# An attention-plus-MLP block rewritten: 512 attention units with 1024-wide exps over three PSUM pairs, one dense slot per unit, MLP in 352-token chunks

## The chip, the cores and the metric

The kernel runs on one core of a Trainium2 chip. The metric is device time of one execution in microseconds; several executions are timed, and the median is quoted. The profile is one execution, recorded by the hardware profiler.

In this text TensorE is PE in the profile (PEld is its weight load), VectorE is DVE, ScalarE is ACT, GpSimd is POOL, and SP issues most transfers. PSUM is the memory that TensorE writes to; the programs hold it as one tensor `ps` of eight banks of 512 columns. "Pitch" is the time from the start of one instruction to the start of the next. A shape like 128x512 is partitions by columns.

## The reference

```python
x = A_x                                   # 1 x 2048 x 1024, bf16
xn = layernorm(x)
# A: attention, 32 heads of 32
q, k, v = split(xn @ wqkv)                # wqkv 1024 x 3072
p = softmax(q @ k.T * 32 ** -0.5)         # 2048 x 2048 per head
s = (p @ v) @ wo                          # wo 1024 x 1024
# B: MLP on a second layernorm of xn
h = gelu(layernorm(xn) @ w1 + b1)         # w1 1024 x 3584, tanh form
g = silu(h @ w2 + b2)                     # w2 3584 x 1024
out = x + s * g
```

Both kernels cut attention into 512 units: four heads, 256 queries, 256 keys. A unit is eight score matmuls (S), the exps of 128 x 2048 scores, and sixteen matmuls for P·V and for the row sums (by a matrix of ones). The MLP and the Q/K/V projections ("dense work") are put between the units on TensorE, so that ScalarE, which has all the exps to do, is never left alone.

## The kernel before

It builds the instruction list of each engine by hand, with semaphore waits. One unit, and the filler of dense work:

```python
ACCB = 5                                   # bank of P.V and row sums
NRING = 5                                  # banks 0-4: scores; banks 6, 7: dense work
...
for kbh in range(2):
    for j in range(4):
        bk = (4 * b + j) % NRING
        ...
            w = [("act_exp", 4 * b - 1)]   # third exp of the unit before is done
        add("tensor", ... en.matmul(bank(bk, kbh * 256, (kbh + 1) * 256), lhsT=KT..., rhs=QT...), ...)
flush(act_pending, b)                      # tanh of earlier MLP items
for j in range(4):
    add("scalar", ... en.activation(Pb[b % NPB][:, j, :], bank(bk), ACT.Exp, scale=SCALE), ...)
if b >= 2:
    emit_pv(b - 2)
run_fillers(mlp_seq, per_batch_ns, None)   # as many dense matmuls as a time budget allows
flush(dve_pending, b)
```

At the end of each group of eight units (256 queries are finished) VectorE normalises straight out of the accumulator bank:

```python
add("vector", lambda en: en.reciprocal(rc_t[ri][:], ps[:, ACCB * 512 + 256:ACCB * 512 + 256 + QW]), ...)
add("vector", lambda en: en.tensor_tensor(OT[:, hg, qb * QW:(qb + 1) * QW],
                                          ps[:, ACCB * 512:ACCB * 512 + QW], rc_t[ri][:], op=ALU.mult), ...)
```

A first-layer MLP item is 256 tokens by two blocks of 128 hidden columns. Its gelu on VectorE: two evictions with bias, square, multiply-add, multiply, and (after tanh on ScalarE) one more; the evictions are 256 columns wide each, the rest 512.

```python
xb = bank + b1                             # L441, twice
u = xb * xb                                # L446
u = u * 0.044715 + 1                       # L448
u = u * xb                                 # L450
th = tanh(0.79788 * u)                     # ScalarE, L456
h = (th + 1) * xb                          # L461
```

The second layernorm's rows are transposed on TensorE and sent through DRAM; the gate is transposed back on TensorE.

The softmax here doesn't subtract the row's maximum and nothing guards it: scores larger than these inputs give would overflow.

## Time and profile before

| | before |
|---|---|
| device time, median of 3 | 1486.78 us |
| first exp starts | 107.0 us |
| 512 units, first exp to last | 1293 us (2.53 us a unit) |
| after the last exp | 86.0 us |
| records of the half-speed TensorE clock | 23, 117.7 us in all |

The first exp, the last and the clock records are read from single instruction times. They cut the run into three stretches. This is the view by windows of these three: the engines' busy time in each, with the granted clock, DMA share and GB/s at the end.

```profile
0.00:107.00 107.00, 54.78 (x652) 40.80 (x656) 57.26 (x113) 19.81 (x23) 32.97 (x38) 1.00 0.51 109
107.00:1400.00 1293.00, 1081.02 (x28992) 723.55 (x28984) 615.80 (x1015) 1121.68 (x2220) 23.08 (x32) 0.96 0.45 102
1400.00:1486.00 86.00, 70.06 (x698) 37.53 (x696) 29.11 (x45) 2.05 (x6) 46.68 (x50) 0.96 0.64 185
```

The columns are window, length, then PE, PEld, DVE, ACT, POOL. In the middle ScalarE is busy 1122 of 1293 us, and no engine is full. So the loss is in waits, spread over engines. The groups view shows what the main instructions cost (busy us, mean ns of one, then idle time of the engine before them and what ended it):

```profile
L695 ACT ACTIVATE Pb<-ps 128x512 bf16<-128x512 f32 x2048 | 1058.7, 609 | 173.2 <-PE ps L686 166.1
L302 PE MATMUL ps<-arena 128*32 128x256 bf16 x14336 | 494.0, 282 | 87.9 <-DMA arena<-in_B_w_dram 66.8
L612 DVE RECIPROCAL rc<-ps 128x256 f32<-128x256 f32 x64 | 112.4, 1756 | 145.8 <-PE ps L605 145.8
L446 DVE TENSOR_TENSOR arena<-arena 128x512 f32<-128x512 f32 x112 | 77.6, 693 | 12.4 <-DVE arena L441 0.9
```

L302 is a helper: its groups are told apart by their tiles; `arena` holds the MLP. ScalarE waits 166 us for scores, TensorE 66.8 us for weights. Twelve microseconds of ScalarE in time order, with idle time in brackets:

```profile
819.62 2.06 ACT L695 ACTIVATE Pb<-ps 128x512 bf16<-128x512 f32 x4
821.54 0.44 ACT L500 ACTIVATE arena<-arena 128x256 f32<-128x256 f32 x1
822.89 6.22 ACT L695 ACTIVATE Pb<-ps 128x512 bf16<-128x512 f32 x12 [0.91 <-PE ps L686]
828.97 0.44 ACT L500 ACTIVATE arena<-arena 128x256 f32<-128x256 f32 x1
829.89 2.06 ACT L695 ACTIVATE Pb<-ps 128x512 bf16<-128x512 f32 x4 [0.48 <-PE ps L686]
```

The best units take 2.06 to 2.08 us (822.89: three units in 6.22 us). Exps of one unit start 477 ns apart, so four take 1.91; the rest, about 155 ns, is the wait of each unit's first exp for scores that may start only after the third exp before.

The transfers of weights, with size and the median time from issue to landing:

```profile
arena<-in_B_w_dram SPq DMA_DIRECT2D x112, 512.0 KB, 4.0
arena<-in_B_w_dram SPq DMA_DIRECT2D x64, 896.0 KB, 6.9
```

### The profile page before, as it was taken

To read this page: it belongs to the slowest core of one execution; us is meant where nothing else is said; L and a number is where in the kernel's file an instruction comes from. 1 tells how busy PE (TensorE), PEld (TensorE's weight loads), DVE (VectorE), ACT (ScalarE), POOL (GpSimd) and SP (SyncE) were. 2 spreads that over 40 slices of the span, in tenths; PEclk is the share of its full clock that TensorE was granted. 3 is DMA by queue.
4 is the path that set the end of the run, shared out by engine and by line. 5 is a ranking of instruction groups with operands and counts; after the bars stand their busy time and mean duration, and the time that the engine had idled before them with its cause. 6 is when DMAs were issued, how large, how long until landed. Compare 5 with 4: busy or idle time off the path is not lost.

```text
span 1486.1 us, 65842 instructions
## 1 busy us (share of the span) xinstructions
PE 1205.9 (81%) x30330; PEld 801.9 (54%) x30336; DVE 702.2 (47%) x1173; ACT 1143.5 (77%) x2246; POOL 102.7 (7%) x119
## 2 busy tenths in 40 slices
PE   2589878887889878987798878988798878777887
PEld 1455656555556545565555555655455655555643
DVE  6532862257422772347522683238522682277233
ACT  1229988897889888988898989988898987687600
POOL 3320000000000100001000100001000000000057
PEclk9999999999999989999899999999999998998999
DMA  6350457125560556045524562165307556535764
GB/s 135 71 129 3 119 119 143 41 60 141 111 144 3 137 123 120 9 101 149 105 52 86 137 158 52 31 145 148 83 5 143 135 163 124 120 116 123 145 198 163
DMA packets 388676, 159.44 MB, mean 107 GB/s; under 512 B 255280, under 2 KB 378160, under 8 KB 388400
## 3 DMA queue, kind: packets, MB, share of 16 engines
q1 hardware_dynamic: 378640, 138.43, 40.6%
q0 software_dynamic: 9760, 16.80, 4.3%
q8 instruction: 238, 3.90, 1.1%
q14 instruction: 38, 0.31, 0.1%
HBM read 142.62 MB, written 12.58 MB: 104 GB/s over the span
## 4 chain that ended last, share of the span: by engine, by line
PE 40%; ACT 18%; DVE 17%; DMA 14%; issue 10%; POOL 1%; DVEq 0%; SPq 0%; ACTq 0%; POOLq 0%
ACT Pb L695 18%; PE ps L302 17%; DMA arena<-in_B_w_dram 13%; PE ps L686 7%; DVE rc L612 6%; PE ps L599 6%; PE ps L605 4%; PE ps L732 3%; DVE arena L441 3%; DVE arena L446 2%; PE ps L269 2%; DVE OT L614 1%; PE ps L383 1%; DVE arena L448 1%; DVE arena L450 1%
## 5 line engine op out<-in xcount | busy, mean ns | idle before, releaser
L695 ACT ACTIVATE Pb<-ps 128x512 bf16<-128x512 f32 x2048 | 1058.7, 609 | 173.2 <-PE ps L686 166.1
L302 PE MATMUL ps<-arena 128*32 128x256 bf16 x14336 | 494.0, 282 | 87.9 <-DMA arena<-in_B_w_dram 66.8
L302 PEld LDWEIGHTS ps<-arena 128*32 128x32 bf16 x14336 | 394.2, 100 | 129.7 <-issue 82.7
L599 PE MATMUL ps<-Pb,Vh 128*32 128x256 bf16 x4096 | 273.8, 285 | 47.9 <-DVE OT L614 38.5
L605 PE MATMUL ps<-Pb,ones 128*32 128x256 bf16 x4096 | 270.1, 281 | 7.8 <-issue 7.7
L686 PE MATMUL ps<-QT,KT 32*128 32x256 bf16 x4096 | 211.5, 280 | 74.5 <-ACT Pb L695 59.0
L599 PEld LDWEIGHTS ps<-Pb,Vh 128*32 128x32 bf16 x4096 | 110.2, 96 | 169.8 <-issue 111.8
L612 DVE RECIPROCAL rc<-ps 128x256 f32<-128x256 f32 x64 | 112.4, 1756 | 145.8 <-PE ps L605 145.8
L686 PEld LDWEIGHTS ps<-QT,KT 32*128 32x128 bf16 x4096 | 61.9, 93 | 219.4 <-ACT Pb L695 186.4
L494 DVE TENSOR_SCALAR arena<-ps,b2h 128x256 f32<-128x256 f32 x64 | 30.9, 482 | 271.9 <-PE ps L302 271.9
L302 PE MATMUL ps<-xnT,wsl 128*32 128x512 bf16 x2048 | 130.8, 388 | 2.1 <-DMA wsl<-in_A_wqkv_dram 2.1
L441 DVE TENSOR_SCALAR arena<-ps,b1T 128x256 f32<-128x256 f32 x224 | 97.9, 479 | 72.7 <-PE ps L302 70.6
L605 PEld LDWEIGHTS ps<-Pb,ones 128*32 128x32 bf16 x4096 | 112.1, 98 | 9.0 <-issue 6.4
L527 POOL DMA_DIRECT2D g_scratch<-arena x16 | 8.9, 558 | 1291.5 <-DVE arena L525 1291.1
L456 ACT ACTIVATE arena<-arena 128x512 f32<-128x512 f32 x112 | 72.3, 646 | 23.9 <-DVE arena L450 23.9
L446 DVE TENSOR_TENSOR arena<-arena 128x512 f32<-128x512 f32 x112 | 77.6, 693 | 12.4 <-DVE arena L441 0.9
L450 DVE TENSOR_TENSOR arena<-arena 128x512 f32<-128x512 f32 x112 | 77.6, 692 | 3.9
L302 PEld LDWEIGHTS ps<-xnT,wsl 128*32 128x32 bf16 x2048 | 55.3, 99 | 41.9 <-issue 6.8
L461 DVE SCALAR_TENSOR_TENSOR arena<-arena 128x512 bf16<-128x512 f32 x112 | 75.1, 685 | 3.4 <-ACT arena L456 3.1
L269 PE MATMUL ps<-ident,arena 128*128 128x128 bf16 x256 | 30.5, 312 | 49.3 <-DVE arena L256 49.3
L383 PE MATMUL ps<-wsl,xnT 128*128 128x128 bf16 x1024 | 67.8, 220 | 0.0
L383 PEld LDWEIGHTS ps<-wsl,xnT 128*128 128x128 bf16 x1024 | 57.4, 98 | 14.2 <-issue 13.8
(47 smaller groups left out, 520.2 us busy)
## 6 DMA issues: line engine op xcount, KB each, us to landing
arena<-in_B_w_dram SPq DMA_DIRECT2D x112, 512.0 KB, 4.0
arena<-in_B_w_dram SPq DMA_DIRECT2D x64, 896.0 KB, 6.9
wsl<-in_A_wqkv_dram POOLq DMA_DIRECT2D x24, 256.0 KB, 6.8
yT_scratch<-arena SPq DMA_DIRECT2D x16, 256.0 KB, 2.8
arena<-yT_scratch SPq DMA_DIRECT2D x8, 512.0 KB, 8.6
g_scratch<-arena POOLq DMA_DIRECT2D x16, 256.0 KB, 2.6
xnT<-in_A_x_dram SPq DMA_DIRECT2D x16, 256.0 KB, 3.0
xnT<-g_scratch SPq DMA_DIRECT2D x16, 256.0 KB, 3.8
```

What stands on the lines that cost most here:

```text
L302: add("tensor", lambda e, j=j: e.matmul(out_fn(j), lhsT=lhsT_fn(j), rhs=rhs, start=start, stop=stop, tile_position=(0, 32 * j), skip_group ...
L383: mms.append((lambda w, inc, DB, dc=dc, tb=tb, t4=t4: add("tensor", lambda e: e.matmul(bank(DB, t4 * 128, (t4 + 1) * 128), lhsT=xnT[:, dc, ...
L441: add("vector", lambda e, k=k, fb=fb: e.tensor_scalar(xb_t[gi][:, k * CW:(k + 1) * CW], bank(DB, k * CW, (k + 1) * CW), b1T[:, fb:fb + 1], ...
L446: add("vector", lambda e: e.tensor_tensor(u_t[gi][:], xb_t[gi][:], xb_t[gi][:], op=ALU.mult), waits=va, inc="gl_b")
L450: add("vector", lambda e: e.tensor_tensor(u_t[gi][:], u_t[gi][:], xb_t[gi][:], op=ALU.mult), waits=[("gl_b", sc.cnt("gl_b"))], inc="gl_u")
L456: add("scalar", lambda e: e.activation(th_t[gi][:], u_t[gi][:], ACT.Tanh, scale=0.7978845608028654), waits=[("gl_u", vu)], inc="gl_t")
L461: add("vector", lambda e: e.scalar_tensor_tensor(hT[:, pi * FBP:(pi + 1) * FBP, :], th_t[gi][:].rearrange("p (k t) -> p k t", k=FBP), 1.0, ...
L599: add("tensor", lambda en, j=j, kb=kb, kbh=kbh, firstg=firstg: en.matmul(ps[32 * j:32 * j + 32, ACCB * 512:ACCB * 512 + QW], lhsT=Vh[i2][: ...
L605: add("tensor", lambda en, j=j, kbh=kbh: en.matmul(ps[32 * j:32 * j + 32, ACCB * 512 + 256:ACCB * 512 + 256 + QW], lhsT=ones[:, 0:32], rhs ...
L612: add("vector", lambda en: en.reciprocal(rc_t[ri][:], ps[:, ACCB * 512 + 256:ACCB * 512 + 256 + QW]), waits=[("pe_pv", b + 1), ("dve_acc", ...
L686: add("tensor", lambda en, j=j, kb=kb, kbh=kbh, bk=bk, qb=qb, i2=i2: en.matmul(bank(bk, kbh * 256, (kbh + 1) * 256), lhsT=KT[i2][32 * j:32 ...
L695: add("scalar", lambda en, j=j, bk=bk, b=b: en.activation(Pb[b % NPB][:, j, :], bank(bk), ACT.Exp, scale=SCALE), waits=[("pe_s", b + 1), ( ...
```

## The change

The kernel was rewritten around a small scheduler that derives waits from named reads and writes. The intent: ScalarE does two wide exps per unit, and everything else is cut so that each unit carries exactly one piece of dense work. The diff is 1350 lines; its core, with cuts marked `...`:

```diff
-        ACCB = 5
-        NRING = 5
-                        bk = (4 * b + j) % NRING
+                bks.append(2 * ((2 * u + j // 2) % 3) + j % 2)      # three pairs of banks, 0-5
+        ACC = 6
+        state = {"bank": 7, "qi": 0}                                # one bank for dense work
...
-                for j in range(4):
-                    ... activation(Pb[b % NPB][:, j, :], bank(bk), ACT.Exp, scale=SCALE)
+            for p in range(2):
+                sl = (2 * u + p) % 3
+                op("scalar", ... activation(pb[:, 2 * p:2 * p + 2, :, :]..., ps[:, sl * 1024:(sl + 1) * 1024], ACT.Exp, scale=SCALE), ...)
...
-                ... en.reciprocal(rc_t[ri][:], ps[:, ACCB * 512 + 256:ACCB * 512 + 256 + QW])
-                ... en.tensor_tensor(OT..., ps[:, ACCB * 512:ACCB * 512 + QW], rc_t[ri][:], op=ALU.mult)
+                op("vector", lambda e: e.tensor_copy(a[:], bank(ACC)), ...)      # bank is free after this
+                for k in range(4):                                  # a quarter in each of four units
+                    dve_tasks[v + k].append(... e.reciprocal(rc[:, k * q4:(k + 1) * q4], a[:, QW + k * q4:...]))
+                dve_tasks[v + 3].append(... "gpsimd" ... e.tensor_tensor(OT..., a[:, 0:QW], rc[:], op=ALU.mult))
...
-    CW = 256
+    CW = 352                                                        # tokens of an MLP chunk
-    run_fillers(mlp_seq, per_batch_ns, None)
+    # one entry of the list per unit: a 128-column block of the first layer, a quarter of a
+    # second-layer item, a Q/K item, a V item or an output item
...
-    u = xb * xb; u = u * 0.044715 + 1; u = u * xb                   # VectorE, 512 wide
+    op("gpsimd", ... e.tensor_tensor(ub, xb, xb, op=ALU.mult))      # 352 wide
+    op("vector", ... e.scalar_tensor_tensor(ub, ub, 1.0 / 0.044715, xb, op0=ALU.add, op1=ALU.mult))
...
-    src = B_w1[:, pi * W1P:(pi + 1) * W1P]                          # 256 columns, 512 KB
-    src = B_w2[:, nb * 128:(nb + 1) * 128]                          # 896 KB
+    src = B_w1[:, k * 512:(k + 1) * 512]                            # 1 MB
+    src = B_w2[:, k * 256:(k + 1) * 256]                            # 1.8 MB
...
+    e.dma_start_transpose(yTc[:, :, 0:n], y_d[t0:t0 + n, :])        # no transposes of y on TensorE
+    e.dma_start_transpose(gres[i4]..., gT_d[:, lo:hi])              # nor of the gate
```

Some lines above are shortened to what they compute. The output projection (48 items) joins the same list, so part of it runs inside the last attention units.

## The prediction

> **What bounds it now.** From the trace's instruction times: first exp at 107.0 us, last ends at 1400.1. So three stretches: 107 us of layernorm and first projections, 1293 us for 512 attention units (2.53 us each), 86 us of tail. The groups view puts the exps (128x512 x2048) at 1058.7 us of busy ScalarE, 173 us idle before them. Start to start, exps of a unit follow at 477 ns, but a unit never takes under 2.08 us: five 512-column banks let the next scores start only after the unit's third exp, so at least 155 ns is lost per unit. Beyond that: every eighth unit 2.7-3.0 us (the 1756 ns reciprocal and 425 ns multiply hold the accumulator bank; 8.8% of the chain of waits in one 100 us window), units with tanh 2.44, and units up to 7.6 us where TensorE waits for weights (66.8 us in the waits view) or VectorE (gelu chain of four 512-wide steps). After each long wait the clock record shows half speed for 3.4 us or more.
>
> **What changes.**
> - Exps: 2 per unit, 1024 wide. A 1024-wide PSUM read on ScalarE took 1023 ns in this trace, a 512-wide exp 605 with pitch 477, so pitch about 905 (estimate), 1.81 us a unit instead of 2.08. The Trainium skill ("ScalarE: Activation LUTs", What ACT_TABLE_LOAD costs) gives 186 ns + 0.833 ns a column, less about 93 overlapped; the trace's pitch is 43 ns lower still. Three PSUM pairs let scores start after the first of the two exps: about 0.3 us slack, so the 155 ns loss goes.
> - TensorE: same columns. From the trace: 102-110 ns per 256-column quad, about 150 for 352. Scores 307, PV 409, dense slot 1.3 us (gelu or Q/K), 1.15 (quarter of w2), 0.92 (V). Unit 2.01, 1.86, 1.64.
> - VectorE: square moves to GpSimd, one step folded. Per w1 unit 0.58+0.53+0.53 us, plus four quarter reciprocals (about 0.55) and a 0.69 us copy per eight units: 2.1 us, also nearly full. Accumulator held 0.7 us instead of 2.2.
> - DMA: six weight passes instead of eight, 1 MB and 1.8 MB pieces with 4 or 8 slots lead, runs twice as long: landing 7 and 9-10 us (estimate from 4.0 and 6.9 us for half sizes) against about 8.6 and 15 us. Hidden.
> - y and gate transposed by DMA. No transposing DMA runs in this trace; "DMA: Bandwidth & Descriptors" (Latency and other measured facts) gives 261 GB/s, so about 3 us per chunk. Hidden unless several times slower.
>
> **Sum.** Per unit, the slower of ScalarE and TensorE: 168 w1 units at 2.15 (tanh adds 345 ns), 192 w2 at 1.9, 84 Q/K and 20 output at 2.01, 48 V at 1.81: 1021 us. Three engines nearly level with in-order queues and one dense bank: add 4%: 1062.
> Start: no y transposes on PE/VectorE, x in 8 queues; LN batches of about 10 us, last projections end near 70 us (now 107).
> Tail: 20 of 48 output items done earlier, no drained MLP: 28 x 1.2 us + PV and stores: 42 us (now 86).
> 70 + 1062 + 42 = about 1175.
>
> **Predicted: 1178 us, 1140 to 1245.** Faster by over 2%: 0.98; within: 0.015; slower: 0.005.
>
> **Right if:** exps 1024 wide, pitch about 905; ScalarE busy about 1000 us, over 90% in the middle; first exp 65-78 us; after the last exp 35-50 us; w1 units near 2.2, w2 near 1.9; DMA wait of matmuls under 20 us; few half-clock events.
> **Wrong if:** transposing DMAs take over 15 us and delay weights, or over 4 us each and bound the tail (they share one queue with in-order waits); VectorE is late with the single dense bank's eviction (w1 units 2.4+); GpSimd squares (1155 ns for 512 columns now) are slow next to VectorE.

## The result

| | before | after |
|---|---|---|
| device time, median of 4 | 1486.57 us | 1197.66 us |
| first exp starts | 107.0 us | 86.7 us |
| 512 units | 1293 us | 1069 us |
| after the last exp | 86.0 us | 37.3 us |
| half-speed clock records | 23, 117.7 us | 3, 8.0 us |

The ratio is 0.8084 (95% interval 0.8028 to 0.8140). Here and below a ratio compares one kernel's runs with those of the kernel before in the same rounds, so it is not quite the ratio of the medians quoted. The prediction of 1178 us, 1140 to 1245, held.

The windows of the three stretches after (columns as above):

```profile
0.00:87.00 87.00, 44.60 (x908) 31.66 (x912) 36.19 (x75) 27.62 (x42) 35.65 (x52) 0.96 0.57 149
87.00:1156.00 1069.00, 1023.12 (x27880) 633.99 (x27872) 595.39 (x1086) 1034.01 (x1240) 199.68 (x231) 1.00 0.38 104
1156.00:1193.00 37.00, 33.23 (x912) 24.72 (x912) 30.85 (x63) 0.00 (x0) 0.73 (x1) 1.00 0.66 163
```

ScalarE is busy 97% of the middle, and TensorE 96%. Of 293 us between the two profiles, 224 came from the middle, 49 from the tail, 20 from the start. The groups after:

```profile
L587 ACT ACTIVATE P<-ps 128x1024 bf16<-128x1024 f32 x1024 | 983.9, 1079 | 31.2 <-PE ps L575 22.0
L302 PE MATMUL ps<-yTc,war 128*32 128x352 bf16 (+1 forms) x5376 | 226.5, 308 | 14.5 <-DVE xb L392 6.9
L621 DVE RECIPROCAL rcs<-accs 128x64 f32<-128x64 f32 x256 | 133.3, 535 | 0.0
L396 DVE SCALAR_TENSOR_TENSOR u<-u,xb 128x352 f32<-128x352 f32 (+1 forms) x168 | 152.8, 909 | 0.0
L394 POOL TENSOR_TENSOR u<-xb 128x352 f32<-128x352 f32 (+1 forms) x168 | 150.0, 893 | 315.7 <-DVE xb L392 285.8
```

ScalarE's wait for scores fell from 166 to 22 us; the wait for weights is gone from these lines (the waits view has one, of 2.7 us). ScalarE in time order now runs without a bracket, tanh between exps:

```profile
154.77 1.95 ACT L587 ACTIVATE P<-ps 128x1024 bf16<-128x1024 f32 x2
156.58 0.53 ACT L399 ACTIVATE th<-u 128x352 f32<-128x352 f32 x1
156.97 1.97 ACT L587 ACTIVATE P<-ps 128x1024 bf16<-128x1024 f32 x2
158.77 0.55 ACT L399 ACTIVATE th<-u 128x352 f32<-128x352 f32 x1
159.16 1.99 ACT L587 ACTIVATE P<-ps 128x1024 bf16<-128x1024 f32 x2
```

Exps start 0.903 us apart (median of single instruction times), so a unit costs ScalarE 1.81 us, and 2.19 with a tanh. The transfers after:

```profile
war<-in_B_w_dram SPq DMA_DIRECT2D x42, 1024.0 KB, 5.4
war<-in_B_w_dram SPq DMA_DIRECT2D x24, 1792.0 KB, 9.4
xnT<-gT_scratch SPq DMA_TRANSPOSE x16, 4.8
yTc<-y_scratch SPq DMA_TRANSPOSE x6, 6.3
```

Twice the bytes land in 1.35 times the time, and a piece now lasts four or eight units.

The units can be sorted by the dense work that TensorE did in them, taking the time from a unit's first exp to the next unit's. Sums over all units of a kind, in us (mean of one in brackets):

| kernel | gelu (168) | second layer (192) | Q/K (84) | V (48) | output (19) |
|---|---|---|---|---|---|
| predicted | 361 (2.15) | 365 (1.9) | 169 (2.01) | 87 (1.81) | 38 (2.01) |
| after | 379 (2.26) | 385 (2.01) | 177 (2.11) | 87 (1.81) | 39 (2.04) |

The prediction added 4% to its sum for coupling and came to 1062 us; 1067 was measured from the first unit's first exp to the last unit's.

### The profile page after: what moved, and what is told of

It reads as the page before. It is cut to its first block, busy times and chain, and to the rows that moved or that the text cites. A ratio compares the mean times of both kernels' runs of the same rounds, so it can differ in the third digit from the quotient of the medians.

```text
span 1193.0 us, 62780 instructions
## 1 busy us (share of the span) xinstructions
PE 1100.9 (92%) x29696; PEld 690.4 (58%) x29696; DVE 662.4 (56%) x1223; ACT 1061.6 (89%) x1281; POOL 236.1 (20%) x284
## 4 chain that ended last, share of the span: by engine, by line
PE 67%; ACT 18%; DVE 10%; DMA 3%; issue 3%; POOL 0%; SPq 0%; POOLq 0%
PE ps L302 40%; ACT P L587 15%; PE ps L575 10%; PE ps L604 10%; PE ps L607 7%; DVE u L396 3%; DVE xb L392 2%; DVE hT L403 2%; ACT th L399 2%; DMA b2h<-in_B_b_dram 2%; DMA war<-in_B_w_dram 1%; ACT xnT L296 1%; DVE rcs L621 1%; DVE stats L245 1%; DVE accs L616 1%
## 5 line engine op out<-in xcount | busy, mean ns | idle before, releaser
L587 ACT ACTIVATE P<-ps 128x1024 bf16<-128x1024 f32 x1024 | 983.9, 1079 | 31.2 <-PE ps L575 22.0
L604 PE MATMUL ps<-P,VP 128*32 128x256 bf16 x4096 | 262.5, 278 | 4.9 <-DVE accs L616 4.2
L607 PE MATMUL ps<-P,ones 128*32 128x256 bf16 x4096 | 257.7, 273 | 3.0 <-issue 3.0
L302 PE MATMUL ps<-yTc,war 128*32 128x352 bf16 (+1 forms) x5376 | 226.5, 308 | 14.5 <-DVE xb L392 6.9
L302 PE MATMUL ps<-hT,war 128*32 128x352 bf16 (+1 forms) x5376 | 230.9, 308 | 8.5 <-issue 8.4
L394 POOL TENSOR_TENSOR u<-xb 128x352 f32<-128x352 f32 (+1 forms) x168 | 150.0, 893 | 315.7 <-DVE xb L392 285.8
L302 PEld LDWEIGHTS ps<-yTc,war 128*32 128x32 bf16 x5376 | 131.5, 96 | 72.6 <-DVE xb L392 16.8
L302 PEld LDWEIGHTS ps<-hT,war 128*32 128x32 bf16 x5376 | 142.1, 97 | 50.9 <-issue 12.0
L396 DVE SCALAR_TENSOR_TENSOR u<-u,xb 128x352 f32<-128x352 f32 (+1 forms) x168 | 152.8, 909 | 0.0
L302 PE MATMUL ps<-xnT,wq 128*32 128x352 bf16 (+2 forms) x2944 | 131.0, 320 | 10.3 <-ACT xnT L296 8.8
L621 DVE RECIPROCAL rcs<-accs 128x64 f32<-128x64 f32 x256 | 133.3, 535 | 0.0
L302 PEld LDWEIGHTS ps<-xnT,wq 128*32 128x32 bf16 x2944 | 77.2, 97 | 39.4 <-ACT xnT L296 8.1
```

Of the source, the lines that this page charges most:

```text
L302: ins = e.matmul(outs(j), lhsT=lhs(j), rhs=rhs, start=start, stop=stop, tile_position=(0, 32 * j), skip_group_check=True)
L394: op("gpsimd", lambda e: e.tensor_tensor(ub[:, 0:n], xb[:, 0:n], xb[:, 0:n], op=ALU.mult), r=[kx], w=[ku])
L396: "vector", lambda e: e.scalar_tensor_tensor(ub[:, 0:n], ub[:, 0:n], 1.0 / 0.044715, xb[:, 0:n], op0=ALU.add, op1=ALU.mult),
L587: op("scalar", lambda e, p=p, sl=sl: e.activation(pb[:, 2 * p:2 * p + 2, :, :].rearrange("p a b q -> p (a b q)"), ps[:, sl * 1024:(sl + 1) ...
L604: e.matmul(bankq(ACC, j, 0, QW), lhsT=VP[vp][:, kb, vo + 32 * j:vo + 32 * j + 32], rhs=pb[:, j, kh, :], start=first, stop=False, tile_posi ...
L607: ins = e.matmul(bankq(ACC, j, QW, 2 * QW), lhsT=ones[:, 0:32], rhs=pb[:, j, kh, :], start=False, stop=last, tile_position=(0, 32 * j), sk ...
```

## The experiments

All results agreed with the reference. The kernel with light weight loads computes with wrong MLP weights: the comparison does not see those weights. "Control" is the changed kernel again.

### Control

> The changed kernel as it is, on the chip that the other three share. Every theory: about 1197 us and a ratio to the kernel before of 0.80 to 0.815, first exp at 87 us, 1067 us of units, tail 37 us. It is the base from which the differences of the other three are taken.

Measured: 1195.88 us, ratio 0.8089 (0.8045 to 0.8132), first exp at 87.7 us, tail 37.2. It is the base for the next three.

### 512-wide exps in the changed kernel

```diff
-            for p in range(2): ... ps[:, sl * 1024:(sl + 1) * 1024] ...
+            for j in range(4): ... activation(pb[:, j, :, :]..., bank(s_bank(u, j)), ACT.Exp, scale=SCALE)
```

> Four exps of 512 columns per unit in place of two of 1024, on the same three PSUM pairs. Theory A (the width is worth the fixed part of two ScalarE instructions per unit, where ScalarE is what a unit waits for): pitch back to 477 ns, 1.91 us of exps per unit instead of 1.81, so plus 0.10 us on the 408 gelu, second-layer and V units and nothing on the 104 Q/K and output units, which TensorE bounds at 2.07 us: about 40 us more than the control, 30 to 50. Rival B (VectorE or TensorE bound most units, the width is off the path): under 10 us more. Rival C (the gain of the change is mostly the wider exps): over 100 us more.

Measured: 1230.71 us, ratio 0.8329 (0.8285 to 0.8374): 35 us over the control. The medians of gelu and V units went from 2.19 to 2.29 and from 1.81 to 1.96; Q/K (2.07) and output (2.07) did not move. Theory A holds: the width is worth 35 us of the 289. The profile line shows a trap:

```profile
L590 ACT ACTIVATE P<-ps 128x512 bf16<-128x512 f32 x2048 | 1074.4, 858 | 14.8 <-PE ps L578 14.4
```

A 512-wide exp "took" 609 ns on average before and 858 here, although they start 477 ns apart in both: with the scores always ready, a record seems to hold time spent behind the instruction before. The traces bear this out: the exps that found ScalarE idle took 597 ns in both kernels (142 before, 13 here). Cost is read from start to start.

### The five-bank ring on top

```diff
+        def s_bank(u, j):
+            return (4 * u + j) % 5          # in place of 2 * ((2 * u + j // 2) % 3) + j % 2
```

> As the run with 512-wide exps, but the scores go through a ring of five PSUM banks as in the kernel before, so the scores of the next unit wait for the third of four exps. Theory A (the ring's slack is worth as much as the width): no unit under 2.08 us, gelu units near 2.44, every hiccup of TensorE or VectorE reaches ScalarE, so 45 to 80 us more than the run with 512-wide exps, 85 to 120 more than the control. Rival B (the extra bank is idle most of the time): the same as the run with 512-wide exps within 10 us.

Measured: 1263.20 us, ratio 0.8543 (0.8486 to 0.8600): 67 us over the control, but only 32.5 over the 512-wide run, under the 45 to 80 expected. The ring does cost (Rival B falls): V units went to 2.08, second-layer units from a mean of 2.07 to 2.17. The miss: gelu units were expected near 2.44 and stayed at a median of 2.29 in both runs. In those a tanh stands between the last exp of one unit and the first of the next, and the wait for scores passes behind it.

### Normalising out of PSUM

```diff
-                op("vector", lambda e: e.tensor_copy(a[:], bank(ACC)), ...)
-                ... four quarter reciprocals, multiply on GpSimd ...
+                op("vector", lambda e: e.reciprocal(rc[:], bank(ACC, QW, 2 * QW)), ...)
+                op("vector", lambda e: e.tensor_tensor(OT..., bank(ACC, 0, QW), rc[:], op=ALU.mult), ...)
```

> The changed kernel, but reciprocal and multiply read the accumulator bank in PSUM in one piece on VectorE as in the kernel before, so the bank is held about 2.2 us instead of 0.7; VectorE has 0.7 us less to do per eight units. Theory A (holding the accumulator stalls TensorE and then ScalarE once per eight units): the first unit after each group end grows from about 2.1 to 2.7 or more, 20 to 80 us more than the control, about 45. Rival B (VectorE's total work is what matters): equal to the control or up to 20 us faster.

Measured: 1241.83 us, ratio 0.8404 (0.8360 to 0.8448): 46 us over the control, with less work on VectorE (653.4 us busy against 662.4 in the changed kernel's profile). By place in the group of eight, the mean of the third unit went from 2.03 to 2.95 us; the other seven moved by no more than 0.17. This is the unit behind whose scores TensorE stands before the next group's first P·V, as the waits view of this run says:

```profile
PE ps L604 <- DVE OT L616: 69.5, 62, 1.9
```

(62 of 64 groups, 1.9 us at most; the changed kernel has 4.2 us in 14 such waits, there for the copy.) Theory A holds: what counted was how long the bank was held, not VectorE's work.

### The square on VectorE

```diff
-                op("gpsimd", lambda e: e.tensor_tensor(ub[:, 0:n], xb[:, 0:n], xb[:, 0:n], op=ALU.mult), ...)
+                op("vector", lambda e: e.tensor_tensor(ub[:, 0:n], xb[:, 0:n], xb[:, 0:n], op=ALU.mult), ...)
```

> The changed kernel, but the square of the gelu is computed on VectorE again instead of GpSimd. In the changed kernel's trace the step after it on VectorE took 1094 ns where GpSimd was at work for most of it and 515 ns where it was not. Theory A (GpSimd's square slows VectorE about as much as it relieves it): that step falls to about 515 ns in all 168 gelu units, VectorE works about 2.5 us per gelu unit in both kernels, and the time is the control's plus 0 to 25 us. Rival B (the prediction's picture: VectorE is relieved by 0.5 us per gelu unit, and is full): gelu units grow from 2.26 to 2.7 or more, 70 to 100 us more than the changed kernel.

Measured: 1206.39 us, ratio 0.8106 (0.8078 to 0.8135), against 0.8084 and 0.8089 for the changed kernel: at most some 10 us slower, and not clear of the intervals. Gelu units sum to 386 us (control 380). Theory A holds. The two steps in question, on VectorE in this run (to be read against L396 and L394 above):

```profile
L396 DVE SCALAR_TENSOR_TENSOR u<-u,xb 128x352 f32<-128x352 f32 (+1 forms) x168 | 92.9, 553 | 0.0
L394 DVE TENSOR_TENSOR u<-xb 128x352 f32<-128x352 f32 (+1 forms) x168 | 86.3, 514 | 5.8
```

Together 1067 ns on VectorE, against 909 for the one step with GpSimd at work. So moving the square away relieved VectorE by 0.16 us per item, not by the half microsecond that the prediction counted. In the changed kernel's trace, of the 352-wide L396 steps those with over 600 ns of GpSimd work beside them took a median of 1094 ns (95 of them), and those with none 517 (5; 517 again for 125 of them in this run). The Trainium skill says so ("SBUF — State Buffer", Who interferes with whom): a VectorE instruction with two inputs in SBUF contends with a GpSimd instruction that reads SBUF. The trace agrees.

### The bias wait at the start

```diff
-        op("vector", lambda e: e.tensor_scalar_mul(b2h[:], b2h[:], 0.5), r=["b2"], w=["b2"])   # third on VectorE
         ... layernorm and first projections ...
         load_piece(0)
         load_y(0)
+        op("vector", lambda e: e.tensor_scalar_mul(b2h[:], b2h[:], 0.5), r=["b2"], w=["b2"])
```

In the changed kernel's start the groups view has this line:

```profile
L239 DVE TENSOR_SCALAR b2h<-b2h 128x8 f32<-128x8 f32 x1 | 0.2, 172 | 20.0 <-DMA b2h<-in_B_b_dram 20.0
```

VectorE, which takes its instructions in order, stood for 20 us at a step of 0.2 us whose input, 4 KB, was issued among the 4 MB of `x` and took 18.2 us to land, while the first tile of `x` had landed at 3.4 us. In the kernel before that load took 6.1 us and the step waited 7.8.

> The changed kernel, but the halving of the second bias, which is VectorE's third instruction and waits for a small load that lands at 20 us, is moved behind the whole layernorm stage. Theory A (this one wait delays the statistics, whose first input is there at 3.4 us, and with them the first exp, which came at 87 us against the predicted 65 to 78): first exp at 68 to 75 us, the time 12 to 19 us below the changed kernel, ratio to the kernel before about 0.798. Rival B (TensorE's projections and GpSimd's normalisation bound the start whatever the statistics do): first exp at 82 us or later, at most 5 us gained.

Measured: 1180.99 us, ratio 0.7947 (0.7924 to 0.7970), first exp at 70.8 us. Theory A holds: this one wait was 16 of the 17 us by which the prediction's start (70 us) was too early.

### Wide exps alone in the kernel before

```diff
-        ACCB = 5
+        ACCB = 6
-                    self.db = 6 + i % 2
+                    self.db = 7
-                    w = [("db_free", i - 1) if i > 1 else None] + ...
+                    w = [("db_free", i) if i > 0 else None] + ...
 ... scores to three pairs of banks, two exps of 1024 columns, waits counted to match ...
```

> The kernel before with only one part of the change: two exps of 1024 columns per unit over three PSUM pairs, so that one bank is left for dense work instead of two. Theory A (exps and ring are worth about 0.27 us per unit only where nothing else holds the unit; the gelu chain on VectorE, the accumulator hold and the waits for weights stay, and one dense bank makes VectorE's delays worse): units of the projection stretches 1.81 to 2.1 us, in all 20 to 90 us less than the kernel before, ratio 0.94 to 0.985. Rival C (exps and their banks are the change): 140 us less or more, ratio 0.905 or below.

Measured: 1653.29 us, ratio 1.1111 (1.1062 to 1.1159). Both theories fall: this part of the change alone makes the kernel 11% slower. ScalarE's wait for scores grew from 166.1 to 412.7 us, and the waits view shows a kind of wait that neither full kernel has at this size:

```profile
ACT Pb L695 <- PE ps L686: 412.7, 296, 35.2
PE ps L302 <- DVE arena L441: 96.5, 84, 3.0
PE ps L302 <- DVE arena L494: 54.5, 59, 2.6
```

Three pairs and an accumulator leave one bank for dense work. TensorE must now wait between any two dense items until VectorE has evicted the first; behind it in order stand the next scores, and ScalarE idles. (The first of the two L302 lines is 3.5 us in the kernel before.) The bank is not alone to blame: of the 212 us that TensorE stood at dense work for VectorE, VectorE spent 49 in the reciprocal out of PSUM and the multiply behind it, steps that the changed kernel no longer has there. The changed kernel has the same single bank and hardly waits (6.9 us for the gelu's evictions).

### Dense slots shifted by half

```diff
         for q in queue:
             for x in q:
+                mid = (x[1] + x[2]) // 2
+                flat += [(x[0], x[1], mid) + x[3:], (x[0], mid, x[2])]
-            if state["qi"] < total:
+            for _half in range(1 if u == 0 else 2):      # two halves per unit, one in the first
```

> The changed kernel, but every dense slot is cut in the middle: a unit runs the second half of one slot and the first half of the next, so that a dense item now ends in mid-slot and the next one starts right behind it on the same single bank. Same instructions, same sums. The kernel before with wide exps alone was 11 per cent slower, with TensorE waiting for VectorE's evictions in mid-slot. Theory A (one dense bank is enough only because scores and PV, 0.7 us of TensorE, stand between the end of an item and the start of the next and hide its eviction): TensorE waits about 0.7 us in every gelu, Q/K, V and output unit and in every fourth unit of the second layer: gelu and Q/K units 2.7 us or more, 120 to 280 us more than the changed kernel, ratio 0.89 to 1.0. Rival B (the eviction overlaps whatever the order): within 20 us of the changed kernel.

Measured: 1453.58 us, ratio 0.9841 (0.9784 to 0.9898): 256 us over the changed kernel, with the same instructions. Gelu units went to 2.92 us in the mean, Q/K to 2.84, V to 2.50. Theory A holds. Two lines of the waits view, which in the changed kernel are 6.9 us in 15 waits and 22.0 us in 24:

```profile
PE ps L302 <- DVE xb L392: 114.3, 167, 0.7
ACT P L591 <- PE ps L579: 263.6, 371, 2.4
```

Over all kinds of dense work TensorE stood 239 us for evictions, and 7 in the changed kernel. The timeline shows the mechanism. First TensorE in the changed kernel, two Q/K units, then VectorE's evictions (CAST) in the same stretch:

```profile
286.06 1.37 PE L302 MATMUL ps<-xnT,wq 128*32 128x352 bf16 x32
287.36 0.40 PE L575 MATMUL ps<-QT,KT 32*128 32x256 bf16 x8
287.69 0.29 PE L604 MATMUL ps<-P,VP 128*32 128x256 bf16 x4
287.81 0.28 PE L607 MATMUL ps<-P,ones 128*32 128x256 bf16 x4
287.91 0.28 PE L604 MATMUL ps<-P,VP 128*32 128x256 bf16 x4
288.02 0.28 PE L607 MATMUL ps<-P,ones 128*32 128x256 bf16 x4
288.13 1.37 PE L302 MATMUL ps<-xnT,wq 128*32 128x352 bf16 x32
```

```profile
287.48 0.53 DVE L326 CAST QT<-ps 128x352 bf16<-128x352 f32 x1 [0.50 <-PE ps L302]
287.92 0.54 DVE L621 RECIPROCAL rcs<-accs 128x64 f32<-128x64 f32 x1
289.55 0.52 DVE L326 CAST QT<-ps 128x352 bf16<-128x352 f32 x1 [1.09 <-PE ps L302]
```

The eviction runs from 287.48 to 288.01, while TensorE does scores and P·V from 287.36 to 288.13, in other banks. When the next dense item starts, the bank is free. In the shifted kernel (two V units) the item ends in mid-slot and TensorE has nothing else to do:

```profile
299.78 0.28 PE L302 MATMUL ps<-wq,xnT 128*32 128x256 bf16 x4
300.60 0.62 PE L302 MATMUL ps<-wq,xnT 128*32 128x256 bf16 x16 [0.53 <-DVE VP L342]
```

The lost time at each item is 0.5 us of bracket here; the start-to-start gap of 0.82 also holds the last matmuls' own time.

### Light weight loads in the kernel before

```diff
+                    k = DC if gp < 2 else 1
-                    add("sync", lambda e: e.dma_start(w1p[gp % 2][:], src), ...)
+                    add("sync", lambda e: e.dma_start(w1p[gp % 2][:, 0:k, :], src[:, 0:k, :]), ...)
 ... the same for w2, with k = 4 of 28 ...
```

> The kernel before with weight loads cut to an eighth (first layer) and a seventh (second layer) after the first two of each; the result is wrong on purpose, the instructions of the compute engines are the same. It takes away the waits for weights, 66.8 us in the waits view of the kernel before. Theory A (these waits and the half-speed clock after them are on the path): 60 to 110 us less than the kernel before, few half-clock stretches left, ratio 0.925 to 0.96. Rival B (VectorE's gelu chain takes their place): less than 25 us gained, ratio over 0.983.

Measured: 1395.19 us, ratio 0.9392 (0.9370 to 0.9413): 89 us less than the kernel before, half-clock records down from 23 to 10 (more than the few that were expected). Theory A holds. The wait for weights, in the kernel before and in this run:

```profile
PE ps L302 <- DMA arena<-in_B_w_dram: 66.8, 58, 5.3
PE ps L302 <- DMA arena<-in_B_w_dram: 0.6, 2, 0.4
```

These waits were on the path, and taking them away was worth more than their 66.8 us; half-speed time also fell, from 117.7 to 73.9 us, and the tail from 86.0 to 78.8, but how the rest divides between the two was not separated. The Trainium skill ("TensorE: Matmul & The Clock Gate", Part 1) describes a clock that falls to half after an idle window of about 3.4 us and returns after a busy one; the records agree in length, each being 3.4, 6.8 or 10.2 us long but for the last, which the end of the run cuts off. But TensorE was not wholly idle before them: in the 3.4 us before each of the 23 records of the kernel before, its matmul records fill from 0 to 54% of the time.

### Chunks of 256 tokens

```diff
-    CW = 352
+    CW = 256
```

> The changed kernel with chunks of 256 tokens instead of 352. Theory A (352 is the width at which the dense work is cut into no more slots than there are units: 256 makes 640 slots of projection and MLP for 512 units, each too short to fill TensorE beside ScalarE): the attention units get shorter, 1000 to 1030 us in all instead of 1069, but 128 MLP slots and all 48 output items are left for the tail, which grows from 37 to 180 to 240 us: in all 90 to 170 us more than the changed kernel. Rival B (352 is worth only its fewer passes over the weights): the tail stays under 60 us and matmuls wait for weights by 30 us or more.

Measured: 1336.11 us, ratio 0.9047 (0.8984 to 0.9111). The units shrank to 1028 us in all, the tail grew to 217.6 us, matmuls waited 20.4 us for weights. Theory A holds. 352 is the width at which the dense work has about as many pieces as there are units (492 and 20 output items, for 512), each about as long as ScalarE's share.

### A better start

```diff
+        ln(0); transpose batch 0
         for b in range(NT // 4):
             ... K items and first V item of batch b ...
+            ln(b + 1)
             ... other V items ...
+            transposes of batch b + 1
             ... Q item of batch b ...
```

with the bias step moved as above.

> The changed kernel with the bias halving moved behind the layernorm, and with the transposes of the next layernorm batch issued ahead of the current batch's Q projection, so that TensorE does not wait 2.5 us three times for ScalarE's copies. Theory A (those three waits and the half-speed clock after them are on the path of the start): first exp at 59 to 65 us instead of 70.8 with the bias alone, the time about 1172 us, ratio 0.785 to 0.792, faster than both kernels. Rival B: first exp at 69 us or later, no gain over the run with the bias moved alone.

Measured: 1171.18 us, ratio 0.7932 (0.7886 to 0.7978), first exp at 60.7 us. It is the fastest kernel: 26 us under the changed one by medians. Against the run with the bias alone (1180.99, another job) the ratios' intervals overlap; the first exp, 10 us earlier in the profile, and the medians speak for Theory A. The ratio came out just above the 0.785 to 0.792 expected.

## Why the prediction was right

**The sum per unit was right, by the right reason in most terms.** The exp pitch was predicted 905 ns and measured 903; taking the width back cost 35 us, against 40 worked out before that run. V units were predicted 1.81 and measured 1.81. The tail came to 37.3 us (42 predicted). DMA waits and half-clock stretches all but vanished, as said. The parts of its sum came to 1174 us, and the profile to 1193.0: 17 more in the start, 7 more in the units, 5 less in the tail.

**The start was mis-sized: 70 us predicted, 86.7 measured.** The prediction's step "x in 8 queues; LN batches of about 10 us, last projections end near 70 us" overlooked a wait that the profile before already showed, at 7.8 us: VectorE's bias step behind a small load. The changed kernel issues all of `x` at once (16 transfers by 10 us, where the kernel before had issued 8), and the load landed later; that the one caused the other was not tested. The wait became 20.0 us, and moving the step gave back 16.

**"VectorE: square moves to GpSimd" was mis-sized.** The step after it was put at 0.53 us, and took 0.91 because GpSimd was reading beside it. The prediction had this only under "wrong if" (the 1155 ns that it gives there is an addition on GpSimd in the old tail, not a square). It explains only part of why gelu units took 2.26 us and not 2.15: with the square back on VectorE they were no faster. The median gelu unit took 2.19, which is two exps and a tanh on ScalarE: a tanh took 387 ns from its start to the next exp's, where 345 had been counted. The rest, 13 us in all, lies in 24 of the 168 units, those over 2.3 us; in 14 of these GpSimd also multiplies for the normalisation.

**Second-layer and Q/K units were about 0.1 us dearer than predicted** (2.01 for 1.9, 2.11 for 2.01). Units without a tanh had medians of 1.81 and 2.07. The excess lies in part in that 0.06 us of the Q/K units, but more in the 59 units of both kinds in which the tanh of an earlier item falls, and in 17 of over 2.3 us. In 16 of these TensorE stood still for 0.3 to 2.0 us that the profile puts to "issue", that is, to no wait that it shows; the cause of that stays open. The 4% kept for coupling was 41 us, and 46 were needed (1067 for 1021). That the allowance fitted is partly luck, since these terms were not in it.

**What the prediction did not see** is the condition for it all. It costed one dense bank as a risk of late evictions. The runs show it to be the hinge: the old kernel with wide exps, one bank and unaligned items is 11% slower (late VectorE steps have a share in that), and the new kernel with its slots shifted by half loses 256 us. The alignment of items with units was not run by itself in the old kernel; in the new one it is what lets a single dense bank do, and so leaves room for the three pairs.

The parts taken back one at a time (35 for width, 32 more for the ring, 46 for the accumulator, 256 for the alignment) do not add up to 289, since they share waits; nor does the 89 us for weights, measured in the old kernel. No run takes back the tail's 49 us. That the DMA transposes are off the path is read from the profile alone: no wait of over 1.3 us names them. The Trainium skill's 261 GB/s ("DMA: Bandwidth & Descriptors", Latency and other measured facts) gave the prediction an estimate of 3 us per chunk; a chunk of 704 KB took 6.3 us from issue to landing, 114 GB/s with all latency, and was still hidden.

## What to carry to other kernels

Where engines work through their instructions in order, place the end of each work item so that the engine's next instructions use other banks for as long as the eviction takes; here a single bank then did the work of two, and the bank saved made room for another engine's wider instructions. Test a part of a rewrite by itself before trusting it: the most visible part here, alone, costs 11%. And look at the first few instructions of each in-order engine for a step that waits for a small transfer.

## What the Trainium skill lacked or had wrong

- "ScalarE: Activation LUTs" (What ACT_TABLE_LOAD costs): its 186 ns + 0.833 ns a column fits the medians (605 ns for 512 columns, 1046 for 1024, against 612 and 1039). With its overlap of about 93 ns for back-to-back instructions the pitch would be about 520 and 946 ns; it was 477 and 903, 43 lower.
- "SBUF — State Buffer" (Who interferes with whom) names the contention with GpSimd, and that the later of the two waits for the other's whole instruction, but gives no figure for this pair: a 352-column step with two inputs went from 517 to 1094 ns beside a GpSimd multiply of 893 that had started 270 ns earlier (median of 95).
- "DMA: Bandwidth & Descriptors" (Latency and other measured facts) gives a transposing DMA's bandwidth, not its latency: 4.8 us for 256 KB and 6.3 us for 704 KB from issue to landing.
- "TensorE: Matmul & The Clock Gate" (Part 1) does not say how idle a window must be: before the 23 half-speed records here TensorE's matmul records filled 0 to 54% of 3.4 us.
- None of the pages that we read says that a ScalarE record can grow at an unchanged pitch: the same 512-wide exp was 609 ns in the mean in one kernel and 858 in another, at a pitch of 477, and 597 wherever it found ScalarE idle.
